# ELU's min/add on GpSimd in place of VectorE, later loads issued by SyncE, and GpSimd casts in halves

## The chip, the cores and the metric

The kernel runs on one core of a Trainium2 chip. The core's engines each work through their own list of instructions in order and wait for each other by semaphores: TensorE (PE in the profile; PEld is its weight loads), VectorE (DVE), ScalarE (ACT), GpSimd (POOL) and SyncE (SP, which here only issues DMA transfers). The metric is device microseconds of one execution. Times below are medians of several executions. A "run" is an experiment: one kernel, executed several times beside the kernel before on the same chip.

## The reference, cut to what matters

```python
# q, k, v: [8 batches, 8 heads, 576, 64] fp32
q_s = softmax(q, axis=-1); k_s = softmax(k, axis=2)       # written out with exp and sums
kv  = einsum('bhsd,bhse->bhde', k_s, v)
x   = einsum('bhsd,bhde->bhse', q_s, kv)  -> [4608, 512]
h   = x @ w_in                                            # [4608, 2048]
g   = where(h > 0, h, exp(minimum(h, 0)) - 1)             # ELU
out = g @ w_out                                           # [4608, 512] fp32
```

Two large matrix products with ELU between them, fed by a small linear attention. The kernel uses that ELU is `max(h, min(exp(h), 1) - 1)`.

## The kernel before

The rows are done in nine blocks of 512. A block has eight groups; a group is eight 128x512 matmuls into one buffer of 128x1024 in PSUM, the memory that TensorE writes its products to, then ELU, then a slice of `GT`, which the second product reads ("out-matmuls"). Attention is cut into 16 units, spread between the groups of blocks 0 to 6. A small scheduler in the kernel (plain Python, at build time) simulates all engines with a table of costs in nanoseconds and fixes each engine's order of instructions from that. Those orders are static: they are fixed when the kernel is built.

```python
def hg(self, j, g, ps, key, how):            # one group of block j
    S.add("pe", 8 * t_f32r(512), mm, ...)    # 8 matmuls into PSUM buffer ps
    esb = self.ESB[i]                        # two such SBUF buffers in turn
    S.add("act", t_act(1024, True), lambda e: e.activation(esb[:, :], P[:, :], AF.Exp), ...)
    if how == "p":                           # dormant: no group uses it
        S.add("gp", 1050, lambda e: e.tensor_scalar(
            esb[:, :], esb[:, :], 1.0, 0.0, ALU.min, ALU.max), ...)
        S.add("dve", t_dve(1024) + 90, lambda e: e.scalar_tensor_tensor(
            gt, esb[:, :], -1.0, P[:, :], ALU.add, ALU.max), ...)
    elif how == "a":                         # ScalarE: relu(1 - exp)
        S.add("act", t_act(1024, False), lambda e: e.activation(
            esb[:, :], esb[:, :], AF.Relu, bias=1.0, scale=-1.0), ...)
        S.add("dve", ..., lambda e: e.scalar_tensor_tensor(
            gt, P[:, :], 0.0, esb[:, :], ALU.max, ALU.subtract), ...)
    else:                                    # "d": VectorE does both steps
        S.add("dve", t_dve(1024, 2) + 80, lambda e: e.tensor_scalar(
            esb[:, :], esb[:, :], 1.0, -1.0, ALU.min, ALU.add), ...)
        S.add("dve", t_dve(1024) + 90, lambda e: e.tensor_tensor(
            gt, esb[:, :], P[:, :], ALU.max), ...)
# ...
# program(): blocks 0 and 1 alternate "da"[g % 2]; blocks 2 to 8 use "d".
# PSUM buffers: three in turn in block 0, then two (g % 2).
# All loads of q, k, v from unit 2 on are issued by GpSimd, which also casts V to bf16
# (1152 elements a partition) and the transposed q from fp16 to the matmul's type.
```

The softmax here doesn't subtract the row's maximum and nothing guards it: scores larger than these inputs give would overflow.

Of the kernel before, what the change touches and what calls it, by code (L numbers as in the profile page):

```python
# [4 lines left out]
ALU = mybir.AluOpType  # L5
# [6 lines left out]
B, H, S, D = 8, 8, 576, 64  # L12
# [5 lines left out]
CH = 9  # L18
# [225 lines left out]
def t_act(n, psum):  # L244
    return n / 1.2 + (90 if psum else 105)


def t_dve(n, fast=1):
    return n / 0.96 / fast + 75


def t_f32r(n):
    return (n + 33) / 2.4


class Gen:
# [100 lines left out]
    def stage1(self, n, key, vconv="gp"):  # L357
        S = self.S
        i = n % 2
        q, k, VB = self.RAW[i]["q"], self.RAW[i]["k"], self.VB[i]  # L360
        v, vname = self.raw("v", n)
        flat = lambda t: t[:, :, :, :].rearrange("p h c d -> p (h c d)")
        S.add("act", t_act(1152, False), lambda e: e.activation(flat(q), flat(q), AF.Exp),  # L363
              key - 3, X=[f"qR{i}"])
        ek = self.ek(i)
        S.add("act", t_act(1152, False), lambda e: e.activation(  # L366
            ek[:, :, :, :].rearrange("p h c d -> p (h c d)"), flat(k), AF.Exp),
            key - 2, X=[f"kR{i}"])
        hs = slice(0, 2) if vconv == "gp" else slice(0, 1)
        eng, t = ("gp", 1250) if vconv == "gp" else ("dve", t_dve(576) + 60)  # L370
        S.add(eng, t, lambda e: e.tensor_copy(  # L371
            VB[:, hs, :, 0:D], v[:, hs, :, :]), key - 50, R=[vname], W=[f"VB{i}"])
        self.conv = S.ops[-1]
        if vconv != "gp":
            S.add("act", t_act(576, False), lambda e: e.activation(
                VB[:, 1:2, :, 0:D], v[:, 1:2, :, :], AF.Copy), key - 50, R=[vname],
                W=[f"VB{i}x"])
            self.conv2 = S.ops[-1]
        S.add("dve", t_dve(1152) + 60, lambda e: e.tensor_reduce(  # L379
            self.ZQ[i][:, :, :].rearrange("p h c -> p (h c)"),  # L380
            q[:, :, :, :].rearrange("p h c d -> p (h c) d"), AX.X, ALU.add),
            key - 3, R=[f"qR{i}"], W=[f"ZQ{i}"])
        S.add("dve", 250, lambda e: e.reciprocal(self.RZQ[i][:, :, :], self.ZQ[i][:, :, :]),
              key - 3, R=[f"ZQ{i}"], W=[f"RZQ{i}"])
        rz = self.RZQ[i][:, :, :].unsqueeze(3).broadcast_to([128, 2, CH, D])
        qso = self.QS[self.alt(n)][:, :, :].rearrange("p c (h d) -> p h c d", h=2)
        S.add("dve", t_dve(1152) + 60, lambda e: e.tensor_tensor(  # L387
            qso, q[:, :, :, :], rz, ALU.mult),
            key - 3, R=[f"qR{i}", f"RZQ{i}"], W=[f"QS{self.alt(n)}"])
# [40 lines left out]

    def widen(self, n, key):
        i, T = n % 2, self.qsT[self.alt(n)]
        self.S.add("gp", 1200, lambda e: e.tensor_copy(  # L433
            T[:, :, :].rearrange("p c t -> p (c t)"),
            self.QT[:, :, :].rearrange("p c t -> p (c t)")),
            key, R=["QT"], W=[f"qsT{self.alt(n)}0", f"qsT{self.alt(n)}1"])

    def side(self, ps, key, *parts):

# [39 lines left out]
    def ao_mm(self, n, x, ps):  # L479
        i = n % 2  # L480
        P, M, T = self.PS[ps], self.MBLK[i], self.qsT[self.alt(n)]
        c0, c1 = self.part(n, x)
        n_ = (c1 - c0) * 64

        def mm(e):
            for f in range(2):
                for h in range(2):
                    hs = slice(h * 64, h * 64 + 64)
                    last = e.matmul(P[:, h * 512:h * 512 + n_], M[hs, f, :],  # L489
                                    T[hs, c0:c1, f * 64:f * 64 + 64], start=(f == 0), stop=(f == 1))  # L490
            return last
        return (2 * t_f32r(n_) + 200, [f"qsT{self.alt(n)}{y}" for y in (0, 1)] +
                [f"MBLK{i}{y}" for y in ("", 0, 1)], mm)

    def xt(self, n, x, ps, key, eng="act"):
# [36 lines left out]
    def hg(self, j, g, ps, key, how):  # L532
        S = self.S
        P = self.PS[ps]
        banks = [f"b{2 * ps}", f"b{2 * ps + 1}"]
        rc = BLK * (j % 3)
        xs = [f"X{kc}_{(8 * j + x) % (RING // 64)}" for kc in range(4) for x in range(8)]

        def mm(e):
            for t in range(2):  # L540
                tt = 2 * g + t
                for kc in range(4):
                    last = e.matmul(P[:, t * 512:(t + 1) * 512],  # L543
                                    self.W1[:, kc, tt * 128:(tt + 1) * 128],
                                    self.XT[:, kc, rc:rc + BLK], start=(kc == 0), stop=(kc == 3))
            return last
        S.add("pe", 8 * t_f32r(512), mm, key, R=xs + [f"W1_{g // 2}"], X=banks)
        self.last_hg = S.ops[-1]
        i = self.eslot % len(self.ESB)
        self.eslot += 1  # L550
        esb = self.ESB[i]
        S.add("act", t_act(1024, True), lambda e: e.activation(esb[:, :], P[:, :], AF.Exp), key,  # L552
              W=[f"E{i}"], X=banks)
        gw = [f"G{j % 2}_{g}"] + (self.early(g) if j == 1 else [])
        gt = self.GT[j % 2][:, 2 * g:2 * g + 2, :].rearrange("p c t -> p (c t)")
        if how == "p":
            S.add("gp", 1050, lambda e: e.tensor_scalar(
                esb[:, :], esb[:, :], 1.0, 0.0, ALU.min, ALU.max), key, X=[f"E{i}"])
            S.add("dve", t_dve(1024) + 90, lambda e: e.scalar_tensor_tensor(
                gt, esb[:, :], -1.0, P[:, :], ALU.add, ALU.max), key,  # L560
                R=[f"E{i}"], W=gw, X=banks)
        elif how == "a":
            S.add("act", t_act(1024, False), lambda e: e.activation(  # L563
                esb[:, :], esb[:, :], AF.Relu, bias=1.0, scale=-1.0), key, X=[f"E{i}"])
            S.add("dve", t_dve(1024) + 90, lambda e: e.scalar_tensor_tensor(  # L565
                gt, P[:, :], 0.0, esb[:, :], ALU.max, ALU.subtract), key,
                R=[f"E{i}"], W=gw, X=banks)
        else:
            S.add("dve", t_dve(1024, 2) + 80, lambda e: e.tensor_scalar(  # L569
                esb[:, :], esb[:, :], 1.0, -1.0, ALU.min, ALU.add), key, X=[f"E{i}"])  # L570
            S.add("dve", t_dve(1024) + 90, lambda e: e.tensor_tensor(  # L571
                gt, esb[:, :], P[:, :], ALU.max), key,
                R=[f"E{i}"], W=gw, X=banks)
# [38 lines left out]
    def program(self):  # L612
        S = self.S
# [49 lines left out]
        def due(n):  # L663

            return when[n][1] + 4 if n in when else 3 + 4 * (n % 2)
# [30 lines left out]
        def loads(*tn):  # L696
            def go():
                for t, n in tn:
                    if n < NU:
                        self.load(n, t, due(n) - 20)  # L700
            return 0, go

        steps = [[first(2)], [wide(2), kv(2), loads(("q", 4), ("k", 4))],
# [16 lines left out]
        def piece(blocks):  # L720
            if steps:
                for n, go in steps.pop(0):
                    go()

        def paced(s):
            S.gate = self.last_hg
            for n, go in slots.pop(s, ()):
                go()
            S.gate = None

        key = 0
        turns = [0, 2, 1]
        for g in range(8):
            self.hg(0, g, turns[g % 3], key, "da"[g % 2])
            key += 1
            if g >= 5:
                piece(0)
# [7 lines left out]
        while steps:  # L745
            piece(1)
        for g in range(8):
            self.hg(1, g, 2 if g == 0 else g % 2, key, "da"[g % 2])
            paced(8 + g)
            if g >= 2:  # L750
                for ts in range(2):
                    self.out_mm(1, ts, 4 + ts, 2 * g - 4, 2 * g - 2, key)
            key += 1
# [4 lines left out]
                    work.append((j, ts, 4 + ts % 2, jj, jj + 8))  # L758
        for j in range(2, NBLK):
            for g in range(8):  # L760
                self.hg(j, g, g % 2, key, "d")
                paced(8 * j + g)
                if j > 2 or g % 3:
                    w = work.pop(0)
                    self.out_mm(*w, key)
                    if w[4] == 16:
                        self.out_store(w[0], w[1], w[2], key + 1)
                key += 1
# [45 lines left out]
```

## Time and profile before

| | before |
|---|---|
| time, all executions beside the change's | 318.13 us median of 4 (317.04 to 321.39) |
| span of the profiled execution | 317.2 us |
| 128x512 matmul, start to start in clean stretches | 227 ns, so eight take 1.81 us |

From the page of the kernel before: the span, each engine's busy time and share, the chain of waits that ended last (by engine), and four groups of instructions (line, engine, operation, tiles, shapes and count, then busy us, mean ns, and idle us before).

```profile
span 317.2 us, 4708 instructions
PE 305.3 (96%) x1997; PEld 239.8 (76%) x1997; DVE 209.2 (66%) x244; ACT 162.3 (51%) x190; POOL 67.0 (21%) x80
...
PE 81%; DVE 7%; ACT 4%; DMA 4%; SPq 0%; issue 0%; POOL 0%
...
L569 DVE TENSOR_SCALAR ESB<-ESB 128x1024 f32<-128x1024 f32 x64 | 60.7, 948 | 68.4 <-ACT ESB L552 68.1
L571 DVE TENSOR_TENSOR GT<-ESB,PS 128x1024 fp32r<-128x1024 f32 x64 | 78.2, 1222 | 2.2
...
L371 POOL CAST VB<-VR 128x1152 bf16<-128x1152 f32 x15 | 18.5, 1232 | 27.8 <-DMA VR<-in_v_dram 27.8
...
L433 POOL CAST qsT<-QT 128x1152 fp32r<-128x1152 f16 x10 | 12.1, 1214 | 30.4 <-PE PS L459 27.7
```

TensorE is the bound, and GpSimd 21% busy. VectorE's min/add (L569) averages 948 ns, but its median in the trace is 695. The timeline of the kernel before shows why (start us, duration us, engine, line, operation; in brackets idle us before and what ended it). Here and in all timelines below, lines of no interest are left out, some without a mark:

```profile
120.30 1.36 DVE L387 TENSOR_TENSOR QS<-QR,RZQ 128x1152 f16<-128x1152 f32 x1
...
121.17 0.72 POOL L329 DMA_DIRECT2D KR<-in_k_dram  x1 [5.33 <-PE PS L459]
121.58 3.81 DVE L569 TENSOR_SCALAR ESB<-ESB 128x1024 f32<-128x1024 f32 x1
121.89 1.16 POOL L433 CAST qsT<-QT 128x1152 fp32r<-128x1152 f16 x1
...
122.98 0.70 POOL L329 DMA_DIRECT2D QR<-in_q_dram  x1
...
123.67 1.16 POOL L371 CAST VB<-VR 128x1152 bf16<-128x1152 f32 x1
...
125.42 1.22 DVE L571 TENSOR_TENSOR GT<-ESB,PS 128x1024 fp32r<-128x1024 f32 x1
126.56 0.16 DVE L468 RECIPROCAL RZK<-PS 128x2 f32<-128x2 f32 x1
126.70 2.12 PE L543 MATMUL PS<-XT,W 128*128 128x512 f32 x8 [0.17 <-DVE GT L571]
```

VectorE's 0.69 us pass lasts 3.81 us across GpSimd's issues and casts, and TensorE then waits. That is what the change sets out to remove. (VectorE's pass reads and writes SBUF, the on-chip memory of all engines; the prediction calls this kind of pass "two-port".)

### The profile page before, as it was taken

The numbers are of one execution on the slowest core, as the hardware profiler recorded it, in microseconds if no ns is written. First come the engines' busy times: TensorE is split into PE (matmuls) and PEld (weight loads), VectorE is DVE, ScalarE is ACT, GpSimd is POOL, SyncE is SP. The second block draws the span as 40 slices with busy tenths as digits, with TensorE's granted clock in tenths as the row PEclk, the third lists the DMA queues.
The fourth block names the chain that finished last, engine by engine and source line by source line (L and its number), as shares of the span: only waits on it lengthen the run. The fifth ranks groups of instructions, "written<-read, shape, count | busy, mean of one in ns | idle before, by whom it ended". The sixth has DMA issues, their size and how long they took to land.

```text
span 317.2 us, 4708 instructions
## 1 busy us (share of the span) xinstructions
PE 305.3 (96%) x1997; PEld 239.8 (76%) x1997; DVE 209.2 (66%) x244; ACT 162.3 (51%) x190; POOL 67.0 (21%) x80
## 2 busy tenths in 40 slices
PE   7789999989999999999999999999999999999995
PEld 7567777767777777776777778787878888888873
DVE  3837853987989859696978778764644554455500
ACT  4738758889666364452637363634343433433311
POOL 0770233234423525050323221201000000000000
PEclk9979999999999999999999999999999999999999
DMA  7899999576587695738282925131111111221122
GB/s 269 296 392 388 390 389 305 185 274 175 188 248 205 155 265 116 212 88 225 64 253 58 244 68 132 35 70 33 35 33 34 35 34 37 51 47 33 33 66 66
DMA packets 29525, 49.39 MB, mean 156 GB/s; under 512 B 13888, under 2 KB 13888, under 8 KB 29504
## 3 DMA queue, kind: packets, MB, share of 16 engines
q0 software_dynamic: 10272, 33.16, 34.4%
q1 hardware_dynamic: 19232, 15.93, 19.5%
q8 instruction: 15, 0.25, 0.3%
q14 instruction: 6, 0.05, 0.0%
HBM read 36.70 MB, written 9.44 MB: 145 GB/s over the span
## 4 chain that ended last, share of the span: by engine, by line
PE 81%; DVE 7%; ACT 4%; DMA 4%; SPq 0%; issue 0%; POOL 0%
PE PS L581 39%; PE PS L543 38%; PE PS L489 3%; DVE ESB L569 3%; DMA VR<-in_v_dram 2%; DVE GT L571 2%; ACT ESB L552 2%; DMA W<-in_moe_w_in_dram 2%; PE PS L459 1%; ACT ESB L563 1%; DVE QS L387 1%; DVE ZQ L379 1%; SPq L329 0%; ACT XT L511 0%; DVE GT L565 0%
## 5 line engine op out<-in xcount | busy, mean ns | idle before, releaser
L581 PE MATMUL PS<-W,GT 128*128 128x512 f32 x576 | 146.1, 396 | 0.4 <-DVE GT L571 0.4
L543 PE MATMUL PS<-XT,W 128*128 128x512 f32 x576 | 143.9, 395 | 1.9 <-DMA W<-in_moe_w_in_dram 1.1
L543 PEld LDWEIGHTS PS<-XT,W 128*128 128x128 f32 x576 | 108.4, 190 | 27.2 <-DVE GT L565 1.6
L581 PEld LDWEIGHTS PS<-W,GT 128*128 128x128 f32 x576 | 105.6, 188 | 25.5 <-issue 1.9
L552 ACT ACTIVATE ESB<-PS 128x1024 f32<-128x1024 f32 x72 | 73.9, 1026 | 99.3 <-PE PS L543 99.3
L569 DVE TENSOR_SCALAR ESB<-ESB 128x1024 f32<-128x1024 f32 x64 | 60.7, 948 | 68.4 <-ACT ESB L552 68.1
L571 DVE TENSOR_TENSOR GT<-ESB,PS 128x1024 fp32r<-128x1024 f32 x64 | 78.2, 1222 | 2.2
L598 ACT ACTIVATE OSB<-PS 128x512 f32<-128x512 f32 x32 | 19.2, 599 | 37.9 <-PE PS L581 37.9
L379 DVE TENSOR_REDUCE ZQ<-QR 128x18 f32<-128x1152 f32 x16 | 21.6, 1348 | 6.2 <-ACT QR L363 6.2
L329 POOL DMA_DIRECT2D KR<-in_k_dram x14 | 10.2, 727 | 71.4 <-PE PS L459 71.4
L371 POOL CAST VB<-VR 128x1152 bf16<-128x1152 f32 x15 | 18.5, 1232 | 27.8 <-DMA VR<-in_v_dram 27.8
L387 DVE TENSOR_TENSOR QS<-QR,RZQ 128x1152 f16<-128x1152 f32 x16 | 22.9, 1431 | 0.4
L511 ACT ACTIVATE XT<-PS 128x640 fp32r<-128x640 f32 (+5 forms) x32 | 19.7, 619 | 4.9 <-PE PS L489 3.9
L363 ACT ACTIVATE QR<-QR 128x1152 f32<-128x1152 f32 x16 | 18.6, 1163 | 2.5 <-DMA QR<-in_q_dram 2.5
L366 ACT ACTIVATE KR<-KR 128x1152 bf16<-128x1152 f32 x16 | 18.6, 1162 | 2.3 <-DMA KR<-in_k_dram 2.3
L489 PEld LDWEIGHTS PS<-qsT,MBLK 64*128 64x128 f32 x128 | 9.5, 184 | 12.1 <-issue 8.8
L433 POOL CAST qsT<-QT 128x1152 fp32r<-128x1152 f16 x10 | 12.1, 1214 | 30.4 <-PE PS L459 27.7
L489 PE MATMUL PS<-qsT,MBLK 64*128 64x320 f32 (+3 forms) x128 | 16.9, 344 | 1.7 <-ACT XT L511 1.2
L329 POOL DMA_DIRECT2D QR<-in_q_dram x14 | 10.4, 743 | 21.1 <-DVE QS L387 21.1
L565 DVE SCALAR_TENSOR_TENSOR GT<-PS,ESB 128x1024 fp32r<-128x1024 f32 x8 | 9.8, 1224 | 4.3 <-ACT ESB L563 4.3
L329 POOL DMA_DIRECT2D VR<-in_v_dram x14 | 10.2, 728 | 3.3 <-POOL VB L371 3.3
L471 DVE TENSOR_SCALAR MBLK<-PS,RZK 128x64 fp32r<-128x64 f32 x32 | 9.1, 284 | 1.1
(28 smaller groups left out, 73.9 us busy)
## 6 DMA issues: line engine op xcount, KB each, us to landing
out_dram<-OSB SPq DMA_DIRECT2D x64, 128.0 KB, 2.3
QR<-in_q_dram POOLq DMA_DIRECT2D x14, 576.0 KB, 6.2
KR<-in_k_dram POOLq DMA_DIRECT2D x14, 576.0 KB, 5.0
VR<-in_v_dram POOLq DMA_DIRECT2D x14, 576.0 KB, 6.3
W<-in_moe_w_in_dram POOLq DMA_DIRECT2D x4, 1024.0 KB, 8.8
W<-in_moe_w_out_dram POOLq DMA_DIRECT2D x4, 1024.0 KB, 18.9
QR<-in_q_dram SPq DMA_DIRECT2D x2, 576.0 KB, 4.2
KR<-in_k_dram SPq DMA_DIRECT2D x2, 576.0 KB, 7.8
```

Of the source, the lines that this page charges most:

```text
L329: S.add(eng, ISSUE[eng], lambda e: e.dma_start(dst, src), key, W=[name], dma=f"{name}{eng}", nbytes=128 * 4608, follow=self.gpq if chain e ...
L363: S.add("act", t_act(1152, False), lambda e: e.activation(flat(q), flat(q), AF.Exp), key - 3, X=[f"qR{i}"])
L379: S.add("dve", t_dve(1152) + 60, lambda e: e.tensor_reduce(self.ZQ[i][:, :, :].rearrange("p h c -> p (h c)"), q[:, :, :, :].rearrange("p h ...
L387: S.add("dve", t_dve(1152) + 60, lambda e: e.tensor_tensor(qso, q[:, :, :, :], rz, ALU.mult), key - 3, R=[f"qR{i}", f"RZQ{i}"], W=[f"QS{se ...
L489: last = e.matmul(P[:, h * 512:h * 512 + n_], M[hs, f, :], T[hs, c0:c1, f * 64:f * 64 + 64], start=(f == 0), stop=(f == 1))
L511: S.add("act", t_act((h1 - h0) * n_, True), lambda e, dst=dst, src=src: e.activation(dst, src, AF.Copy), key, W=W, X=X)
L543: last = e.matmul(P[:, t * 512:(t + 1) * 512], self.W1[:, kc, tt * 128:(tt + 1) * 128], self.XT[:, kc, rc:rc + BLK], start=(kc == 0), stop ...
L552: S.add("act", t_act(1024, True), lambda e: e.activation(esb[:, :], P[:, :], AF.Exp), key, W=[f"E{i}"], X=banks)
L569: S.add("dve", t_dve(1024, 2) + 80, lambda e: e.tensor_scalar(esb[:, :], esb[:, :], 1.0, -1.0, ALU.min, ALU.add), key, X=[f"E{i}"])
L571: S.add("dve", t_dve(1024) + 90, lambda e: e.tensor_tensor(gt, esb[:, :], P[:, :], ALU.max), key, R=[f"E{i}"], W=gw, X=banks)
L581: last = e.matmul(dst, GT[:, jj, ts * 128:(ts + 1) * 128], self.W2[:, jj, :], start=(jj == 0), stop=(jj == 15))
L598: S.add("act", t_act(512, True), lambda e: e.activation(osb[:, :], src, AF.Copy), key, W=[f"O{i}0", f"O{i}1"], X=[f"b{bk}"])
```

## The change

Its intent: take the min/add off VectorE (where it collides with GpSimd) and off ScalarE, give it to the idle GpSimd, keep GpSimd's other work short (casts in halves) and free of waits (loads of units 6 and later issued by SyncE). Cut to its core:

```diff
         if how == "p":
-            S.add("gp", 1050, lambda e: e.tensor_scalar(
-                esb[:, :], esb[:, :], 1.0, 0.0, ALU.min, ALU.max), key, X=[f"E{i}"])
-            S.add("dve", t_dve(1024) + 90, lambda e: e.scalar_tensor_tensor(
-                gt, esb[:, :], -1.0, P[:, :], ALU.add, ALU.max), key,
+            S.add("gp", 1080, lambda e: e.tensor_scalar(
+                esb[:, :], esb[:, :], 1.0, -1.0, ALU.min, ALU.add), key, X=[f"E{i}"])
+            S.add("dve", t_dve(1024) + 90, lambda e: e.tensor_tensor(
+                gt, esb[:, :], P[:, :], ALU.max), key,
 ... V cast on GpSimd: one instruction of 1152 -> two of 576 (660 ns each in the cost table)
 ... q cast on GpSimd: one of 1152 -> 640 and 512 elements; its readers wait only for the half they read
-                        self.load(n, t, due(n) - 20)
+                        self.load(n, t, due(n) - 20, "gp" if n < 6 else "sp")
-            self.hg(0, g, turns[g % 3], key, "da"[g % 2])
+            self.hg(0, g, turns[g % 3], key, "aapppppp"[g])
-            self.hg(1, g, 2 if g == 0 else g % 2, key, "da"[g % 2])
+            self.hg(1, g, 2 if g == 0 else g % 2, key, "p")
-                self.hg(j, g, g % 2, key, "d")
+                self.hg(j, g, g % 2, key, "p")
```

The first hunk changes the pair of operations, from (min, max) to (min, add). 70 of the 72 groups now use this arm.

More of the change, by code (lines that the diff above doesn't have):

```diff
@@ L368, in stage1 @@
             key - 2, X=[f"kR{i}"])
-        hs = slice(0, 2) if vconv == "gp" else slice(0, 1)
-        eng, t = ("gp", 1250) if vconv == "gp" else ("dve", t_dve(576) + 60)
+        eng, t = ("gp", 660) if vconv == "gp" else ("dve", t_dve(576) + 60)
         S.add(eng, t, lambda e: e.tensor_copy(
-            VB[:, hs, :, 0:D], v[:, hs, :, :]), key - 50, R=[vname], W=[f"VB{i}"])
+            VB[:, 0:1, :, 0:D], v[:, 0:1, :, :]), key - 50, R=[vname], W=[f"VB{i}"])
         self.conv = S.ops[-1]
-        if vconv != "gp":
+        if vconv == "gp":
+            S.add("gp", 660, lambda e: e.tensor_copy(
+                VB[:, 1:2, :, 0:D], v[:, 1:2, :, :]), key - 50, R=[vname], W=[f"VB{i}x"])
+            self.conv = S.ops[-1]
+        else:
             S.add("act", t_act(576, False), lambda e: e.activation(
@@ L432, in widen @@
         i, T = n % 2, self.qsT[self.alt(n)]
-        self.S.add("gp", 1200, lambda e: e.tensor_copy(
-            T[:, :, :].rearrange("p c t -> p (c t)"),
-            self.QT[:, :, :].rearrange("p c t -> p (c t)")),
-            key, R=["QT"], W=[f"qsT{self.alt(n)}0", f"qsT{self.alt(n)}1"])
+        for x, (c0, c1) in enumerate(((0, 5), (5, CH))):
+            self.S.add("gp", 130 * (c1 - c0) + 60, lambda e, c0=c0, c1=c1: e.tensor_copy(
+                T[:, c0:c1, :].rearrange("p c t -> p (c t)"),
+                self.QT[:, c0:c1, :].rearrange("p c t -> p (c t)")),
+                key, R=["QT"], W=[f"qsT{self.alt(n)}{x}"])
     def side(self, ps, key, *parts):
@@ L491, in mm @@
             return last
-        return (2 * t_f32r(n_) + 200, [f"qsT{self.alt(n)}{y}" for y in (0, 1)] +
+        return (2 * t_f32r(n_) + 200, [f"qsT{self.alt(n)}{y}" for y in (0, 1)
+                                       if (c0 < 5, c1 > 5)[y]] +
                 [f"MBLK{i}{y}" for y in ("", 0, 1)], mm)
```

## The prediction

> **What bounds the kernel now.** TensorE. The page has PE busy 305.3 of 317.2 us; the chain of waits that ended last is 81% PE, 7% DVE, 4% ACT, 4% DMA. Busy time overstates matmuls because they overlap, so I read the timeline: in clean stretches eight 128x512 matmuls start every 1.81 us (227 ns each). 1152 of them make 261 us. From the last groups' start to start, the attention matmuls add some 25 us. Before 17.3 us PE waits for inputs, and after the last matmul about 4 us pass.
>
> Start to start between successive matmuls, only these gaps are stalls that an engine caused after 24 us: 0.33 us at 60.8 (waits DVE), 1.39 at 66.3 (ACT), 0.44 at 82.8, 0.33 at 126.7, 0.34 at 143.5, 0.61 at 146.1 (all DVE). Together 3.4 us, 1.1% of the span. Another 1.3 us at 17.9 to 20.4 goes with a granted clock of 0.79, which the change doesn't touch.
>
> **What the change does.**
> - Takes the DVE min/add off DVE: 64 ops, 60.7 us, median 0.695 us. Nine lasted 1.5 to 3.8 us, each while GpSimd was casting or issuing. The Trainium skill ("SBUF — State Buffer", "Who interferes with whom") says a two-port VectorE instruction and GpSimd exclude each other; the trace agrees (3.81 us at 121.6 across a cast and an issue). All three stalls after 120 us follow such an op.
> - Takes six of the eight Relu passes (1.06 us) off ScalarE. They matter in block 1 (53 to 91 us), where ACT and DVE are fullest and three of the six stalls lie.
> - Puts 70 fp32 128x1024 ops on GpSimd. No trace has one. Estimate from the 1152-element cast (1.15 us undisturbed): 1.0 to 1.1 us, so about 75 us more; GpSimd goes from 67 to roughly 120 us with the loads moved. It stays under half busy.
> - VectorE's max keeps 1.22 us: one input is PSUM, and a GpSimd cast beside it at 91.7 us took its normal 1.15. The two-SBUF-input multiply (16 times, 1.36 us) may still collide with GpSimd: one took 1.72 and another 2.19 us before.
> - Halved casts add about 0.1 us each, off the path.
> - Loads of later units leave GpSimd, so their buffer waits (71 us before K loads alone) cannot block ELU; SyncE is idle enough.
>
> **On the critical path.** Exp, min/add, max becomes 1.03 + 1.08 + 1.22 plus hops, about 3.5 us, 0.4 longer than undisturbed before. In blocks 2 to 8 a PSUM buffer returns after 7.26 us and needs about 5.4: hidden. In block 0, three PSUM buffers give 5.44 us against 5.4, two exp buffers 1.8 per group against 1.81: a tie, so no gain and perhaps 0.5 us lost. In block 1, I expect one to two of its 2.2 us back; after 120 us nearly all 1.3 us. Net 2 to 3 us gained.
>
> **Prediction.** 316.6 us, 80% range 313.2 to 321.0. Faster by over 2%: 0.06. Within 2%: 0.86. Slower by over 2%: 0.08.
>
> **What would show it.** GpSimd tensor_scalar groups near 1.08 us; DVE busy 55 to 65 us lower; no stretched DVE op over 2.5 us; matmul gaps near 126 to 146 us gone; total busy PE nearly unchanged; the tail after 298 us the same 14.5 us of matmuls.
>
> **What would make it wrong.** GpSimd's two-operation pass costing 1.6 us or more (block 0 then loses 4 us or more); max and GpSimd excluding each other after all; GpSimd waiting in order on a late V load or transpose with ELU work behind it; output stores or transposes stuck behind loads on SyncE. Faster than my range would need the input phase before 17.3 us to shorten, which nothing here does.

## The result, and the profile after

The kernel after takes 381.03 us (median of 4, 381.03 to 382.54) against 318.13 us: ratio 1.198, 95% interval 1.191 to 1.205. The output is correct.

From the page of the kernel after, the lines that answer to those of before:

```profile
span 379.2 us, 4735 instructions
PE 324.3 (86%) x1997; PEld 243.3 (64%) x1997; DVE 150.3 (40%) x180; ACT 156.6 (41%) x184; POOL 302.4 (80%) x145
...
POOL 48%; PE 27%; ACT 9%; DVE 6%; DMA 4%; issue 3%; POOLq 1%; SPq 0%
...
L562 POOL TENSOR_SCALAR ESB<-ESB 128x1024 f32<-128x1024 f32 x70 | 253.9, 3633 | 45.2 <-ACT ESB L557 44.8
...
L564 DVE TENSOR_TENSOR GT<-ESB,PS 128x1024 fp32r<-128x1024 f32 x70 | 85.5, 1221 | 188.1 <-POOL ESB L562 188.1
```

The moved pass takes 3633 ns, not the 1000 to 1100 predicted. VectorE's max is unchanged at 1221 ns and now waits 188 us for GpSimd. In the trace 69 of the 70 passes take 3.61 to 3.64 us, the other 4.00, whether VectorE is busy or idle beside them. The end of the kernel, where there is no attention left, shows how this reaches TensorE. Timeline of the kernel after:

```profile
339.06 2.14 PE L548 MATMUL PS<-XT,W 128*128 128x512 f32 x8 [0.62 <-DVE GT L564]
...
341.23 1.03 ACT L557 ACTIVATE ESB<-PS 128x1024 f32<-128x1024 f32 x1 [2.17 <-PE PS L548]
...
342.34 7.27 POOL L562 TENSOR_SCALAR ESB<-ESB 128x1024 f32<-128x1024 f32 x2 [0.94 <-ACT ESB L557]
...
346.00 1.22 DVE L564 TENSOR_TENSOR GT<-ESB,PS 128x1024 fp32r<-128x1024 f32 x1 [3.35 <-POOL ESB L562]
...
347.28 2.11 PE L548 MATMUL PS<-XT,W 128*128 128x512 f32 x8 [0.63 <-DVE GT L564]
```

One PSUM buffer goes round once from 339.06 to 347.28: 8.2 us for matmuls, exp, pass (3.63) and max. Two buffers are in turn, so two groups take 8.2 us, while TensorE has only 7.26 us of work for them (32 matmuls of 227 ns).

Where the time went, by stage. A stage runs from the first matmul of one stage to the first of the next in each profiled trace; the last row runs from the last matmul of the last group to the end. The other columns are kernels of the experiments below.

| stage (us) | before | after | min/max everywhere (e1) | ELU back (e3) | last one (e11) |
|---|---|---|---|---|---|
| up to the first group | 17.3 | 18.4 | 18.0 | 18.2 | 17.2 |
| block 0 | 16.4 | 24.5 | 17.9 | 16.5 | 14.9 |
| out-matmuls of block 0, attention | 19.8 | 21.6 | 19.8 | 19.8 | 20.4 |
| block 1 | 26.1 | 35.1 | 26.1 | 26.3 | 26.1 |
| block 2 | 30.5 | 38.0 | 31.1 | 30.5 | 29.5 |
| block 3 | 33.4 | 37.5 | 34.3 | 32.6 | 32.6 |
| blocks 4, 5, 6 | 98.6 | 111.8 | 98.1 | 97.5 | 97.5 |
| blocks 7, 8 | 56.0 | 70.3 | 56.3 | 56.0 | 56.0 |
| end | 19.0 | 22.0 | 19.4 | 19.0 | 19.1 |

The loss is in every block, most (8 to 9 us) where least other work hides it: block 0, where 1.81 us of matmuls a group meet 3.63 us of pass, and block 1.

The turn of the buffers is not all of it. In the late blocks part of the loss stands at the block's start, where the out-matmuls wait for the max of the block before's last group: 2.20 us at 291.24, in block 7. And the page shows a lower granted clock of TensorE, in tenths for 40 slices of the span, before and then after:

```profile
PEclk9979999999999999999999999999999999999999
PEclk9988999879999989999999999999998999899999
```

In the trace of the kernel after the granted clock is 0.50 in seven stretches, 27 us in all, against one of 3.4 us before. Inside them some 48 of the 128x512 matmuls start 427 ns after the one before, not 227, against 6 before. By an estimate from these counts (42 times 0.2 us) up to 8 of the 63 us go with the clock. All four executions show it (mean granted clock 0.955 to 0.964, against 0.984 to 1.000 in the kernel before). e1 and e7, with identical orders and shorter passes, have one such stretch each, at the start (10.2 and 3.4 us long). So the later ones came with the long pass; what brings them about no run shows.

### The profile page after: what moved, and what is told of

It reads as the page before. It is cut to its first block, busy times and chain, and to the rows that moved or that the text cites. A ratio compares the mean times of both kernels' runs of the same rounds, so it can differ in the third digit from the quotient of the medians.

```text
span 379.2 us, 4735 instructions
## 1 busy us (share of the span) xinstructions
PE 324.3 (86%) x1997; PEld 243.3 (64%) x1997; DVE 150.3 (40%) x180; ACT 156.6 (41%) x184; POOL 302.4 (80%) x145
## 4 chain that ended last, share of the span: by engine, by line
POOL 48%; PE 27%; ACT 9%; DVE 6%; DMA 4%; issue 3%; POOLq 1%; SPq 0%
POOL ESB L562 42%; PE PS L548 14%; PE PS L586 11%; DVE GT L564 6%; ACT ESB L557 6%; POOL qsT L437 2%; DMA VR<-in_v_dram 2%; POOL VB L374 2%; POOL VB L370 2%; DMA W<-in_moe_w_in_dram 2%; PE PS L493 1%; POOLq L264 1%; ACT XT L516 1%; ACT QR L363 1%; ACT KR L366 1%
## 5 line engine op out<-in xcount | busy, mean ns | idle before, releaser
L562 POOL TENSOR_SCALAR ESB<-ESB 128x1024 f32<-128x1024 f32 x70 | 253.9, 3633 | 45.2 <-ACT ESB L557 44.8
L548 PE MATMUL PS<-XT,W 128*128 128x512 f32 x576 | 153.4, 412 | 23.1 <-DVE GT L564 21.5
L586 PE MATMUL PS<-W,GT 128*128 128x512 f32 x576 | 152.6, 408 | 19.8 <-DVE GT L564 19.8
L564 DVE TENSOR_TENSOR GT<-ESB,PS 128x1024 fp32r<-128x1024 f32 x70 | 85.5, 1221 | 188.1 <-POOL ESB L562 188.1
L548 PEld LDWEIGHTS PS<-XT,W 128*128 128x128 f32 x576 | 110.9, 198 | 58.7 <-DVE GT L564 32.9
L603 ACT ACTIVATE OSB<-PS 128x512 f32<-128x512 f32 x32 | 19.1, 598 | 56.0 <-PE PS L586 56.0
L370 POOL CAST VB<-VR 128x576 bf16<-128x576 f32 x15 | 11.7, 780 | 8.5 <-DMA VR<-in_v_dram 8.5
L437 POOL CAST qsT<-QT 128x640 fp32r<-128x640 f16 (+1 forms) x20 | 13.1, 669 | 0.0
L374 POOL CAST VB<-VR 128x576 bf16<-128x576 f32 x15 | 11.2, 747 | 0.0
L463 PE MATMUL PS<-VB,KR 64*64 64x65 bf16 x576 | 8.0, 197 | 2.0 <-POOL VB L374 2.0
L420 ACT ACTIVATE qsT<-PS 128x1152 fp32r<-128x1152 f16 (+2 forms) x7 | 6.4, 929 | 7.9 <-PE PS L413 7.9
L463 PEld LDWEIGHTS PS<-VB,KR 64*64 64x64 bf16 x576 | 6.1, 110 | 5.0 <-POOL VB L374 2.2
## 6 DMA issues: line engine op xcount, KB each, us to landing
W<-in_moe_w_out_dram POOLq DMA_DIRECT2D x4, 1024.0 KB, 19.1
```

The lines of the kernel that those rows point to most:

```text
L437: self.S.add("gp", 130 * (c1 - c0) + 60, lambda e, c0=c0, c1=c1: e.tensor_copy(T[:, c0:c1, :].rearrange("p c t -> p (c t)"), self.QT[:, c0 ...
L548: last = e.matmul(P[:, t * 512:(t + 1) * 512], self.W1[:, kc, tt * 128:(tt + 1) * 128], self.XT[:, kc, rc:rc + BLK], start=(kc == 0), stop ...
L562: S.add("gp", 1080, lambda e: e.tensor_scalar(esb[:, :], esb[:, :], 1.0, -1.0, ALU.min, ALU.add), key, X=[f"E{i}"])
L564: S.add("dve", t_dve(1024) + 90, lambda e: e.tensor_tensor(gt, esb[:, :], P[:, :], ALU.max), key, R=[f"E{i}"], W=gw, X=banks)
L586: last = e.matmul(dst, GT[:, jj, ts * 128:(ts + 1) * 128], self.W2[:, jj, :], start=(jj == 0), stop=(jj == 15))
```

## The experiments

Theory A: the whole loss comes from what this pair of operations costs on GpSimd. Rivals: any two-operation pass is that slow (B); it waits for a port into SBUF that VectorE or another engine holds (C); it is the in-place operand (D); it is the loads or halves (E), or the orders, made for a wrong cost (F).

Differences of 1 to 2 us need care: within one kernel the time of an execution goes with its mean granted clock. The kernel before, on the chip of e1 to e8, took 317.1 to 318.2 us at 1.00, 318.5 to 319.1 at 0.995 and 321.7 at 0.984.

### e1: another pair of operations, same orders

```diff
-                esb[:, :], esb[:, :], 1.0, -1.0, ALU.min, ALU.add), key, X=[f"E{i}"])
-            ... e.tensor_tensor(gt, esb[:, :], P[:, :], ALU.max)
+                esb[:, :], esb[:, :], 1.0, 0.0, ALU.min, ALU.max), key, X=[f"E{i}"])
+            ... e.scalar_tensor_tensor(gt, esb[:, :], -1.0, P[:, :], ALU.add, ALU.max)
```

exp is never negative, so the max with 0 does nothing; the -1 rides along in VectorE's max. A comparison of the instruction lists found no other difference on any engine.

> The kernel after the change, with one edit: GpSimd does (min 1.0, max 0.0) in place of (min 1.0, add -1.0), and VectorE's max takes the -1 along as a three-operand instruction. Orders on all engines are identical. Theory A (the pair min/add is itself what is slow on GpSimd, 3.63 us): the pass takes 1.0 to 1.2 us, VectorE's instruction stays 1.22, and the time is 314 to 320 us. Rival B (any two-operation fp32 pass of 1024 elements costs GpSimd 3.6 us): the pass stays at 3.6 and the time at 378 to 384 us. Rival C (it waits for a port that VectorE or another engine holds): the pass stays near 3.6 too, since nothing around it changes.

322.12 us (6 executions, 320.0 to 324.11), ratio to before 1.011 (1.006 to 1.016). Groups of its page:

```profile
L564 DVE SCALAR_TENSOR_TENSOR GT<-ESB,PS 128x1024 fp32r<-128x1024 f32 x70 | 85.4, 1220 | 127.0 <-POOL ESB L562 127.0
L562 POOL TENSOR_SCALAR ESB<-ESB 128x1024 f32<-128x1024 f32 x70 | 74.0, 1056 | 143.8 <-ACT ESB L557 143.8
```

The pair of operations accounts for 59 of the 63 us (381.03 - 322.12 against 381.03 - 318.13). B and C fall: two operations can be fast, and nothing around the pass changed. But e1 is still slower than before, and it is above the range expected for A. So with the predicted cost of the pass in place, the predicted gain was still missing. The runs e6 to e11 deal with that.

### e2: which forms are slow

Before, with 29 GpSimd instructions on dead scratch tiles (an old q and k tile) after GpSimd's last real work, and with blocks 6 and 7 on the "a" arm, so that VectorE runs no two-port pass there. (Twenty in a row, among them a copy twice, and then three of them again three times.)

> The kernel before, with 20 GpSimd instructions on dead scratch added at its end, where GpSimd idles: each another form of the pass, and three of them again beside VectorE's two-port passes. Output right. Theory A: (min, add) in place 3.6 us, (min, max) about 1.1, out of place the same as in place, half the width about half. Rival B (cost grows with the number of operations): (min, max) 3.6 and one operation alone about 1.8. Rival D (reading and writing one tile in place): out of place near 1.1. Rival C (ports): with VectorE using one port, (min, add) falls near 1.1, and beside two-port passes it rises.

Output correct; one execution, 318.74 us. From its timeline, GpSimd alone (a row of several gives the stretch from the first's start to the last's end):

```profile
221.26 2.80 POOL L622 TENSOR_SCALAR QR<-QR 128x1024 f32<-128x1024 f32 x1
224.15 3.33 POOL L621 TENSOR_SCALAR QR<-QR 128x1024 f32<-128x1024 f32 x3
...
227.56 3.64 POOL L621 TENSOR_SCALAR QR<-QR 128x1024 f32<-128x1024 f32 x1
...
235.01 3.65 POOL L621 TENSOR_SCALAR KR<-QR 128x1024 f32<-128x1024 f32 x1
238.74 1.92 POOL L621 TENSOR_SCALAR QR<-QR 128x512 f32<-128x512 f32 x1
240.74 1.04 POOL L621 TENSOR_SCALAR KR<-QR 128x1024 f32<-128x1024 f32 x1
241.87 0.62 POOL L621 TENSOR_SCALAR QR<-QR 128x512 f32<-128x512 f32 x1
242.55 1.04 POOL L638 COPY KR<-QR 128x1024 f32<-128x1024 f32 x1
...
250.72 2.40 POOL L643 TENSOR_TENSOR QR<-QR,KR 128x1024 f32<-128x1024 f32 x1
```

In the order of the program these are mult alone; (mult, add), (add, mult), (mult, mult); (max, min); (min, add) out of place; (min, add) at half width; (min, max) out of place; (min, max) at half width; a copy; and a two-input mult. All forms, ns of one instruction at 128x1024 fp32 from the trace, leaving out those that met a two-port pass of VectorE:

| form | ns |
|---|---|
| (min, max); (mult, add); (add, mult); (mult, mult) | 1043 to 1057 |
| copy, cast to bf16 | 1037 to 1044 |
| min alone; add alone; mult alone | 2775 to 2798 |
| (min, add); (max, min); (add, min) | 3641 to 3645 |
| (min, add) from bf16 to bf16; (min, max) from bf16 to bf16 | 3628; 1042 |
| 512 elements: (min, add); (min, max) | 1922; 617 |

Spans on GpSimd are rough in a profile, but the starts agree: back to back, (mult, add), (add, mult) and (mult, mult) start 1.13 to 1.14 us apart, (max, min) and (add, min) 3.72 to 3.73.

The three levels of cost do not follow the number of operations: one operation alone is 2.6 times slower than the fast pairs, and (max, min) costs 3.6 us where (min, max) costs 1.05. D falls too (3645 out of place). So does C as the cause: among VectorE's two-port passes (205 to 210 and 276 to 295 us) (min, add) took 3.63 to 4.06 us and (min, max) 1.04 to 1.37, so a meeting costs up to 0.4 us, but without any such pass the slow pairs still take 3.64 us. From width 512 to 1024 the slope is 3.36 ns an element for (min, add) and 0.83 for (min, max). Why these pairs and not others no run shows; the runs give only the cost of each form.

### e3: ELU put back, loads and halves kept

```diff
-            self.hg(0, g, turns[g % 3], key, "aapppppp"[g])      # and block 1 "p", blocks 2-8 "p"
+            self.hg(0, g, turns[g % 3], key, "da"[g % 2])        # and block 1 "da", blocks 2-8 "d"
```

> The kernel after the change with ELU's min/add put back on VectorE and ScalarE as before; loads of later units from SyncE and the halved casts stay. Theory A (all of the loss is the GpSimd pass): 315 to 320 us, level with before or up to 2 us faster, as fewer VectorE passes stretch. Rival E (loads from SyncE or halved casts cost the time, through late transposes or stores): over 330 us.

318.27 us (316.48 to 319.82), ratio 0.9985 (0.993 to 1.004): level. E falls: the other two parts cost nothing in the median. Its trace shows what they are worth. VectorE's min/add passes of 1.5 to 3.8 us are gone, none over 1.21 us; the gaps at 126 to 146 us are gone; blocks 3 to 6 take 130.2 us against 132.1. On the other hand its first group starts 0.9 us later than before; e9 takes that up.

### e4: the scheduler told the true cost

```diff
-            S.add("gp", 1080, lambda e: e.tensor_scalar(
+            S.add("gp", 3630, lambda e: e.tensor_scalar(
```

> The kernel after the change, with the kernel's own static scheduler told that the pass takes 3630 ns in place of 1080; so only orders differ. Theory A with GpSimd as the bound: 70 passes of 3.63 us are 254 us, with 36 us of casts and 16 us of issuing, behind a start at 27 us: nothing to win but waits, 355 to 381 us. Rival F (the loss is mainly orders that were made for a wrong cost): under 335 us.

394.34 us (392.1 to 395.82), ratio 1.238. F falls: orders made for the true cost do not help. They even cost 13 us more, outside what was expected. TensorE waits 51 us for VectorE's max there, against 41 in the kernel after, and some 70 matmuls are 427 ns apart against 48, which is an estimated 4 us more; why these orders are worse is not settled.

### e7: a pass of middle length

```diff
-                esb[:, :], esb[:, :], 1.0, 0.0, ALU.min, ALU.max), key, X=[f"E{i}"])    # of e1
+                esb[:, :], esb[:, :], 1.0, None, ALU.min), key, X=[f"E{i}"])
```

> As the min/max kernel of the first set (322.1 us, pass 1.04 us), same orders on all engines, but the GpSimd pass is (min 1.0) alone, which the form test put at 2.78 us; VectorE adds the -1 and takes the max as there. Theory A with buffers as the limit: two groups share two PSUM buffers, and a buffer's turn (matmuls 1.97, exp 1.03, pass, max 1.22, hops about 0.35) is 7.37 us against 7.27 of matmuls, so late blocks lose only what the out-matmuls of a block's end wait (2.4 us at a pass of 3.63, so about 1.6); block 0 loses 4 to 5 us: 338 to 350 us. Rival G (loss in proportion to the pass's length): 322 + 59 * 1.74 / 2.59 = 362 us. Rival H (GpSimd's sum of busy time is the bound): 381 - 70 * 0.85 = 322 us.

346.79 us (344.69 to 348.56), ratio 1.089, pass 2781 ns in the profile:

```profile
L562 POOL TENSOR_SCALAR ESB<-ESB 128x1024 f32<-128x1024 f32 x70 | 194.5, 2781 | 68.6 <-ACT ESB L557 68.5
```

Inside the range of the buffer theory, far from proportional loss (362) and from a bound by GpSimd's summed time (322). Block 0 loses 3.0 us to e1, less than the 4 to 5 expected, and block 7 takes 31.2 us against 29.2 in e1, of which 1.6 us is one wait of the out-matmuls at the block's end for the max of the last group. Eight such waits sum to 12.8 us in this profile, against 2.9 us of them in e1, so they are the largest part of the 23.4 us between the two profiles. This fits a time set by three things: the turn of a PSUM buffer, the rate of block 0, and the wait at each block's end. Block 1 loses 4.6 us, more than any other, and for it no such account was made.

### e6: min/max pass in blocks 2 to 8 only

```diff
-                self.hg(j, g, g % 2, key, "d")      # of e3, with the "p" arm of e1
+                self.hg(j, g, g % 2, key, "p")
```

> The kernel with ELU put back (318.3 us) except that blocks 2 to 8 use GpSimd's 1.04 us min/max pass. Theory I (in the min/max kernel it is collisions with VectorE's two-input multiply and a 0.4 us longer chain at the static order's tight places that cost, in these blocks): 1.5 to 3 us above the kernel with ELU put back, 319.5 to 322. Rival J (what the min/max kernel lost lies in blocks 0 and 1): level with it, 317 to 319.

319.87 us (316.8 to 321.51), ratio 1.004 (0.999 to 1.009): 1.6 us above e3 by the medians, so on the side of theory I, though the difference is about as large as the scatter. By stages it is plainer: the blocks from 3 on take 0.1 to 0.2 us more each than in e3 and the end 0.4, some 1.5 us in all. Nothing is won in these blocks, since with VectorE e3 already has TensorE without gaps there.

### e5 and e8: min/max pass in block 1 only

```diff
-            self.hg(1, g, 2 if g == 0 else g % 2, key, "da"[g % 2])     # of e3, "p" arm of e1
+            self.hg(1, g, 2 if g == 0 else g % 2, key, "dp"[g % 2])     # e5
+            self.hg(1, g, 2 if g == 0 else g % 2, key, "p")             # e8
```

> The kernel with ELU put back, but in block 1 the four groups that had ScalarE's extra Relu pass use GpSimd's min/max pass; the other four stay on VectorE. If ScalarE's load is what stalls block 1 (0.48, 1.39 and 0.44 us), they go: 1 to 2 us below the kernel with ELU put back, 316.0 to 317.5. If GpSimd's casts and its longer chain cost as much there: 318 to 320.

> As the last, with all eight groups of block 1 on GpSimd's min/max pass. No VectorE two-port pass is left to exclude GpSimd there, but the chain is 0.4 us longer in each group: 316 to 319 us, best if the stalls of block 1 were VectorE's; at or above the kernel with ELU put back if two PSUM buffers at 5.4 us against 5.4 us of matmuls are the limit.

e5: 316.59 us (314.6 to 318.98), ratio 0.997 (0.992 to 1.002). e8: 316.80 us (314.57 to 317.94), ratio 0.994 (0.990 to 0.999). Both medians are some 2 us below before; only e8's interval excludes 1. In the traces blocks 1 and 2 together take 56.0 and 55.7 us against 56.8 in e3: about 1 us is what the lighter load of ScalarE and VectorE in block 1 is worth. The rest of the scatter had another source: in these two profiles the first group's matmuls start at 16.7 us (e5) and 19.0 us (e8), although the two kernels differ only in block 1.

### e9, e10, e11: who starts first

In e3 and e5, one V cast of the first unit meets VectorE's two-input multiply. Timelines of e3 and then e5:

```profile
9.86 0.66 POOL L370 CAST VB<-VR 128x576 bf16<-128x576 f32 x1 [8.40 <-DMA VR<-in_v_dram]
10.12 1.61 DVE L390 TENSOR_TENSOR QS<-QR,RZQ 128x1152 f16<-128x1152 f32 x1
10.46 1.80 POOL L374 CAST VB<-VR 128x576 bf16<-128x576 f32 x1
12.21 3.12 POOL L344 DMA_DIRECT2D W<-in_moe_w_in_dram  x4
```

```profile
9.57 0.67 POOL L370 CAST VB<-VR 128x576 bf16<-128x576 f32 x1 [8.10 <-DMA VR<-in_v_dram]
10.17 0.67 POOL L374 CAST VB<-VR 128x576 bf16<-128x576 f32 x1
10.29 1.76 DVE L390 TENSOR_TENSOR QS<-QR,RZQ 128x1152 f16<-128x1152 f32 x1
10.79 3.17 POOL L344 DMA_DIRECT2D W<-in_moe_w_in_dram  x4
```

The Trainium skill ("SBUF — State Buffer", section "Who interferes with whom") says that a VectorE instruction with two SBUF inputs contends with a GpSimd instruction that reads SBUF, and that issue order, not the shape of the operation, decides who blocks. The traces agree: with a V that landed 0.3 us later, the second half starts after the multiply and takes 1.80 us, not 0.67, and the loads of the first weights behind it are issued 1.4 us later. A whole cast, as in before, starts ahead of the multiply (10.13 against 10.29 us) and keeps its 1.15 us. The test makes the multiply wait:

```diff
             qso, q[:, :, :, :], rz, ALU.mult),
-            key - 3, R=[f"qR{i}", f"RZQ{i}"], W=[f"QS{self.alt(n)}"])
+            key - 3, R=[f"qR{i}", f"RZQ{i}"], W=[f"QS{self.alt(n)}"],
+            after=[self.conv0] if n == 1 else ())       # conv0: second half of unit 0's V cast
```

e9 is e8 with it, e10 is e1 with it, e11 is e5 with it.

> The kernel with all of block 1 on GpSimd's min/max pass (316.8 us), plus one wait: VectorE's multiply of unit 1 starts only after GpSimd's two cast halves of unit 0's V. In the profiles of halved casts the second half took 0.67 us where it started before that multiply and 1.80 us where it started after, and the first group's matmuls began at 16.7 to 16.8 us or at 18.0 to 19.0 us. Theory K (who starts first holds the other off, and the W1 loads queue behind the cast): both halves 0.66, the first group at 16.6 to 17.0 us, 314.5 to 316 us. Rival L (the late start is the inputs' landing and only coincides): the first group stays near 18 us in some runs and the median stays at 316.5 to 317.

> The whole change with the pass as (min, max) (322.1 us in the first set), plus the same wait. Theory K: it gains 1 to 2 us by the start and by fewer matmuls at a low clock, 320 to 321 us; what stays above the kernel before lies in the late blocks and block boundaries. Rival L: 321.5 to 323.

> As the first of this set, with only the four groups of block 1 that had ScalarE's Relu pass on GpSimd and the other four on VectorE (316.6 us without the wait). Theory K: 314.5 to 316 us, level with all eight.

| | time, us | ratio to before (95%) | first group at, us | block 0, us |
|---|---|---|---|---|
| e9 | 318.90 (316.98 to 320.52) | 1.002 (0.998 to 1.006) | 16.8 | 14.8 |
| e10 | 321.30 (320.87 to 324.32) | 1.010 (1.006 to 1.014) | 17.1 | 15.3 |
| e11 | 315.32 (314.93 to 317.52) | 0.991 (0.987 to 0.995) | 17.2 | 14.9 |

The start of e11:

```profile
9.80 0.66 POOL L370 CAST VB<-VR 128x576 bf16<-128x576 f32 x1 [8.33 <-DMA VR<-in_v_dram]
10.40 0.67 POOL L374 CAST VB<-VR 128x576 bf16<-128x576 f32 x1
11.02 3.17 POOL L344 DMA_DIRECT2D W<-in_moe_w_in_dram  x4
11.11 1.36 DVE L390 TENSOR_TENSOR QS<-QR,RZQ 128x1152 f16<-128x1152 f32 x1 [0.99 <-POOL VB L374]
```

In all three profiles both halves take 0.66 to 0.67 us and the first group starts at 16.8 to 17.2 us, so theory K holds for the start. In e9 V landed so early (second half at 9.92 us) that the wait was hardly needed; in e10 and e11 the half started at 10.30 and 10.40, where the multiplies without the wait started at 10.11 to 10.34. Only the profiled execution of each was traced, so "always" is not shown. Block 0 is less clear: the scheduler fills TensorE's idle time before the first group with dummy matmuls, and with the wait's simulated times it put in 103, not 87. So the wait alone is not shown to be what keeps matmuls of block 0 from half rate in these three, though e5 and e6 also ran it at full rate, with 87. For the totals the expectation held in e11 alone. e10 gained 0.8 us by the median, just under the 1 to 2 expected. e9 got worse: the new wait changed the scheduler's simulated times, so orders differ throughout, and TensorE now waits 1.84 us at 82.6 us, behind a GpSimd pass that met the same kind of multiply. Its timeline:

```profile
79.03 1.36 DVE L390 TENSOR_TENSOR QS<-QR,RZQ 128x1152 f16<-128x1152 f32 x1
79.17 2.12 POOL L563 TENSOR_SCALAR ESB<-ESB 128x1024 f32<-128x1024 f32 x1 [4.40 <-ACT ESB L558]
...
82.60 2.12 PE L549 MATMUL PS<-XT,W 128*128 128x512 f32 x8 [1.84 <-DVE GT L565]
```

The pass takes 2.12 us where it takes 1.04 undisturbed. (This profile is of e9's fastest execution. e8 has a pass of 2.25 us too, at 74.1 us, and TensorE does not wait after it: what counts is where the meeting falls.) e1 has the same: 1.40 and 1.70 us, the second followed by a wait of 1.44 us of TensorE.

e11 beats both kernels, before by 0.9% (interval above), and not by its clock alone: at a granted clock of 0.999 or more it took 314.9 to 315.2 us, and before, on the same chip, 317.1 and 318.4. It has the loads on SyncE and the halved casts of the change, ELU on VectorE as before except for the four groups of block 1 that had ScalarE's Relu pass, which use the (min, max) pass, and the multiply's one wait.

## Why the prediction was wrong, point by point

- **The step that failed** is "Puts 70 fp32 128x1024 ops on GpSimd ... Estimate from the 1152-element cast ...: 1.0 to 1.1 us". The pass takes 3.63 us (253.9 us in all, where 75 were predicted). e1 shows that this is 59 of the 63 us: with another pair of operations and identical orders the pass takes 1.04 us. The estimate took the cost of one kind of instruction for that of another because both read and write one tile of like size. e2 shows that on GpSimd the operations decide, by a factor of 3.5. The prediction named this under what would make it wrong, and set "1.6 us or more" as the limit, but gave slower only 0.08. It also passed over a possible hint in the diff: the change did not keep the pair of the dormant arm.
- **What followed from it** was computed rightly in kind. "In blocks 2 to 8 a PSUM buffer returns after 7.26 us and needs about 5.4: hidden": the need became 8.2 us with the long pass, and the two groups then took 8.2. e7 puts a pass of 2.78 us where this says it should be. Left out were the waits at a block's end (2.20 us in block 7) and the matmuls at a low clock (up to 8 us in all); "total busy PE nearly unchanged" failed with them, at 324.3 against 305.3 us.
- **"Net 2 to 3 us gained" would have been wrong even with the pass at 1.04 us**: e1 is 1.1% slower than before. Two terms had the wrong size. The late blocks, called "hidden", lose about 1.5 us (e6 against e3). In e1, blocks 2 and 3 alone lose 2.3 us against e3, by a stretched pass (1.70 us, and a wait of 1.44 behind it) and a wait of 1.26 us at a block's end. And "Halved casts add about 0.1 us each, off the path" fails at the start, where the second half is on the path and can lose a race with VectorE: 1.80 against 0.67 us, and a first group at 18.0 to 19.0 us, not 16.7 to 17.2 (e1, e3, e8 against e5, e6, e9 to e11).
- **Block 1, "one to two of its 2.2 us back"**: about 1 us against e3 in e5, e8 and e11 for blocks 1 and 2 together (0.6 to 1.0 against before), nothing in e1, e9 and e10.
- **Right**: TensorE was the bound. The three gaps after 120 us were VectorE's passes stretched by GpSimd, and went with them in e3 (1.9 us over blocks 3 to 6). VectorE's max kept 1.22 us beside GpSimd. SyncE took the loads without harm. VectorE's busy time fell by 59 us. Once the pass is short, "perhaps 0.5 us lost" fits block 0: 15.3 us in e10 against 14.8 in e9, both at full clock.
- **Open**: why some pairs are fast and single operations are not; why e4's orders are worse; and what makes the granted clock low, later in the kernel after as well as at the start of block 0. At the start it was 0.50 from 18 to 20 us in before and from 20 to 22 us in e8, and 1.00 there in e5. In the profiles with a first group at 17.3 us or later matmuls of block 0 ran at half rate, in those at 17.2 or earlier none did; that is a coincidence of two things, not a test. By blocks 0 of e8 and e5 it is worth 1.7 us.

## What to carry to other kernels

Before moving an elementwise pass to another engine, measure that very instruction there, with its own operations, on scratch data in a profile; here a copy of like size took 1.04 us and (min, add) 3.63, and the neighbouring pair (min, max) was 3.5 times cheaper. Once the pass is cheap, ask what it gains: an engine that is already hidden gives nothing back, and a longer chain still costs at the places where a static order has no slack. Where two engines hold each other off, as VectorE's multiply and GpSimd's cast did here (0.67 us became 1.80), an instruction split in two has a second start at which to lose the race, so order the pair explicitly where it lies on the path.

## What the Trainium skill lacked or had wrong

- "GPSIMD Engine Reference", section "Engine selection", says that one-input elementwise work there is roughly at line rate. That holds for (min, max), (mult, add), (add, mult), (mult, mult), copy and cast (1.04 to 1.06 us for 1024 fp32 elements), not for (min, add), (max, min), (add, min) at 3.63 to 3.65 us, nor for min, add or mult alone at 2.78 to 2.80 us. The page has no table by operation.
- The same page, section "Performance versus the Vector engine", gives 1.03 cycles an element for bodies of up to two operations. The slope of (min, max), 0.83 ns an element, agrees within 3% at the 1.2 GHz that the page states. That of (min, add) is 3.36 ns, four times as much, also with two operations.
- "SBUF — State Buffer", section "Who interferes with whom", was right here, with numbers it lacks: a 0.67 us cast became 1.80 us and a 1.04 us pass 2.12 us behind VectorE's two-input multiply, and the multiply went from 1.36 to 1.76 us (2.19 in before) when it came second.
